# First chunks of x and w1 in three transfers, two chunks multiplied term by term, and a mask loaded from GpSimd's queue

## The chip, the cores and the metric

The program runs on one core of a Trainium2 chip. The metric is the device time of one execution in microseconds, as the median of several runs. The core has five engines that run their own instruction streams and wait for each other by semaphores: TensorE (PE, matrix products; PEld is its weight load), VectorE (DVE), ScalarE (ACT), GpSimd (POOL) and SyncE (SP), which here only issues transfers. Sixteen DMA engines move the data.

## The reference

With x of 2048 rows and 448 columns, the block mixes a linear attention and a squared-ReLU network by a gate of each row:

```python
g = sigmoid((x * gate_w).sum(-1, keepdims=True))
# A: 16 heads of 28 columns; phi(t) = where(t > 0, t + 1, exp(t)) + 1e-6
q, k, v = heads(x @ wqkv)
kv, z = sum_s phi(k)[s] v[s]^T, sum_s phi(k)[s]
a = ((phi(q) @ kv) / (phi(q) @ z + 1e-6)) @ wo
# B: 448 -> 1792 -> 448
b = relu(x @ w1 + b1) ** 2 @ w2 + b2
out = g * a + (1 - g) * b
```

## The kernel before, in words

Each operand of a product is split into a high part (a copy to PE's 32-bit type `fp32r`, `split_hi`) and a low part (the rest, a subtraction, `split_lo`), and a product is the sum of three terms: high by high, high of w1 by low of x, low of w1 by high of x. The 448 rows of the contraction are cut into four chunks of 128 rows; the last chunk holds the same 64 rows twice, so that two terms do for it.

The hidden layer is computed transposed: a tile of 128 hidden units (f) by 512 rows of x (a block b) needs 11 matmuls of 512 columns, three for each of chunks 0 to 2 and two for chunk 3. The first four tiles (`first`, f = 0 to 3 of block 0) are filled side by side, chunk by chunk, in lines 537 to 560, while x and w1 are still arriving. Everything after that is a long hand-written order on PE, ACT and DVE (`manual_schedule`): tiles of the up projection, of the down projection, key products, sums over keys, and in the second half the queries and the attention. `up_chunk` writes the three terms of one tile and one chunk; its last argument picks a single term.

The start goes like this. PE runs 14 matmuls on constants (line 177) whose result nobody reads. SP issues two transfers `xwr` of 256 KB, each with 256 columns of x's chunk 0 and 256 columns of w1's chunk 0, then x and w1 of chunks 1, 2 and 3 in turn, 256 KB each (`xr`, `w1r`), then biases and further weights. Of chunk 0, ACT makes the high part of x and DVE that of w1, half by half; PE multiplies halves of 256 columns of x with the first two tiles of w1 (line 547), then tiles 2 and 3 with all 512 columns, then the other two terms. Chunks 1 to 3 are split whole by ACT (high) and DVE (low), and PE does all terms of a tile before the next tile.

Transfers take their destinations from one ring of 15 slots (`slot`), and a transfer waits until the slot's last user is done. SP's transfers also take turns on eight semaphores, so that each waits for the landing of the eighth before it. Near the middle, `key_sums` builds `zk` on POOL and `load_kv` loads a mask `kvm` and four pieces of wv on SP's queue; `kv_product` needs the mask in line 406. POOL's own queue carries the rearranging transfers `qr` (line 474) and `m_s`.

Of the kernel before, what the change touches and what calls it, by code (L numbers as in the profile page):

```python
# [7 lines left out]
F = mybir.dt.float32  # L8
# [7 lines left out]
P = 128  # L16
TB = 512
# [8 lines left out]
def f32(ap):  # L26
    return ap.bitcast(F)


@with_exitstack  # L30
def gated_mix_kernel(ctx: ExitStack, tc: tile.TileContext, xw, xt, xn, wk, wq, wv, wo, w1a, w1b, w2, b1, b2, gw,
                     hmask, kvmask, halves, out):
    nc = tc.nc
    act, dve, pool, pe, sp = nc.scalar, nc.vector, nc.gpsimd, nc.tensor, nc.sync
# [13 lines left out]
    def bank(name):  # L48
        turn[0] ^= 1
        return ms_p.tile([P, 512], F, name=name, tag=f"ms{turn[0]}")  # L50
# [3 lines left out]
    def slot(shape, dt, name):  # L54
        return work.tile(shape, dt, name=name, tag="s", bufs=NSLOT)

    def load(dst, src):
        sp.dma_start(out=dst, in_=src)
# [4 lines left out]
    def split_hi(eng, hi, src):  # L63
        if eng is act:
            act.activation(hi, src, AF.Copy)  # L65
        elif eng is pool:
            pool.tensor_scalar(hi, src, 1.0, 0.0, op0=ALU.mult, op1=ALU.add)
        else:
            eng.tensor_copy(hi, src)  # L69

    def split_lo(eng, lo, src, hi):
        eng.tensor_tensor(lo, src, f32(hi), op=ALU.subtract)  # L72
# [29 lines left out]
    x_raw, xs = {}, {}  # L102
# [5 lines left out]
    def new_x(b):  # L108
        return [keep.tile([P, 4, TB], R, name=f"x{p}{b}", tag=f"x{p}", bufs=2) for p in "hl"]

    def split_x(b, c):
        if c == 0:
            xs[b] = new_x(b)
        (xh, xl), r = xs[b], x_raw[b, c]
        if c < 3:
            split_hi(act, xh[:, c], r)
            split_lo(dve, xl[:, c], r, xh[:, c])
        else:
            split_last(xh[:, 3], xl[:, 3], r, side)
# [9 lines left out]
    w1_s, w1_raw = {}, {}  # L129
# [5 lines left out]
    def new_w1(h, g):  # L135
        n, a, z = ((TB, 0, 16), (3 * P, 48, 0))[g]
        w = keep.tile([P, a + 7 * n + z], R, name=f"w1_{h}{g}", tag=f"w1{g}", bufs=1)
        w1_s[h, g] = w[:, a:a + 7 * n].rearrange("p (c n) -> p c n", c=7)
        return w1_s[h, g]

    def split_w1(h, g, c):
        if c == 0:
            new_w1(h, g)
        split_w(w1_s[h, g], c, w1_raw.pop((h, g, c)), act, dve)
# [7 lines left out]
    def split_w2(f):  # L152
        w2_s[f] = keep.tile([P, 2, D], R, name=f"w2_{f}", tag="w2", bufs=NH)
        split_hi(act, w2_s[f][:, 0], w2_raw[f])
        split_lo(dve, w2_s[f][:, 1], w2_raw.pop(f), w2_s[f][:, 0])
# [26 lines left out]
    dve.memset(side[64:], 1.0)  # L182

    xw_raw = []
    for n in range(2):
        xw_raw.append(slot([P, TB], F, f"xwr{n}"))
        load(xw_raw[n], xw[n])
    for c in range(1, 4):
        load_x(0, c)
        load_w1(0, 0, c)  # L190
# [27 lines left out]
    def up_chunk(ps, b, f, c, only=None):  # L218
        h, fl = divmod(f, NH)
        g, i = divmod(fl, 4)  # L220
        w, cols = w1_s[h, g], slice(i * P, (i + 1) * P)
        xh, xl = xs[b]
        if c < 3:
            terms = [(w[:, c, cols], xh[:, c]), (w[:, c, cols], xl[:, c]), (w[:, 4 + c, cols], xh[:, c])]
        else:
            terms = [(w[:, 3, cols], xh[:, 3]), (w[:, 3, cols], xl[:, 3])]
        for n, (a, m) in enumerate(terms):
            if only in (None, n):
                pe.matmul(ps, a, m, start=(c == 0 and n == 0), stop=(c == 3 and n == 1))  # L229
# [155 lines left out]
    kv, wv_s, kvm = [], [], []  # L385

    def load_kv(c):
        if c == 0:
            kvm.append(slot([JE, D], F, "kvm"))
            load(kvm[0], kvmask)  # L390
        wv_s.append(slot([P, D], F, f"wv{c}"))
        load(wv_s[-1], wv[c])

    def kv_product():
        kv_ps = bank("kv_ps")
        z_ps = mm_p.tile([P, 512], F, name="z_ps", tag="mm")
        for c in range(4):
            pe.matmul(z_ps[:, 2 * c:2 * c + 2], zks[0][:, c].rearrange("p j r -> p (j r)"), ones, start=True,  # L398
                      stop=True)
        dve.tensor_copy(zc, z_ps[:, 0:8:2])  # L400
        for j in range(NJ):
            js = slice(j * JE, (j + 1) * JE)
            for c in range(4):
                pe.matmul(kv_ps[:JE, js], wv_s[c][:, js], gsum[c][:, js], start=(c == 0), stop=(c == 3))  # L404
        raw = slot([JE, D], F, "kv_raw")
        dve.tensor_tensor(raw, kv_ps[:JE, :D], kvm[0], op=ALU.mult)
        return raw.rearrange("p (j k) -> p j k", j=NJ)
# [126 lines left out]

    first = [mm_p.tile([P, 512], F, name=f"h_ps0_{f}", tag="mm") if f < 2 else bank(f"h_ps0_{f}") for f in range(4)]
    for c in range(4):
        if c == 0:
            xs[0] = new_x(0)  # L540
            w, (xh, xl) = new_w1(0, 0), [x[:, 0] for x in xs[0]]
            sides = slice(0, TB // 2), slice(TB // 2, TB)
            for n, cols in enumerate(sides):
                split_hi(act, xh[:, cols], xw_raw[n][:, sides[0]])
                split_hi(dve, w[:, 0, cols], xw_raw[n][:, sides[1]])
                for f in range(2):
                    pe.matmul(first[f][:, cols], w[:, 0, f * P:(f + 1) * P], xh[:, cols], start=(n == 0), stop=False)  # L547
            for m, (lo, hi) in enumerate(((xl, xh), (w[:, 4], w[:, 0]))):
                for n, cols in enumerate(sides):
                    split_lo(dve, lo[:, cols], xw_raw[n][:, sides[m]], hi[:, cols])  # L550
        else:
            split_x(0, c)
            split_w1(0, 0, c)
        if c == 0:
            for n in range(3):
                for f in range(0 if n else 2, 4):
                    up_chunk(first[f], 0, f, c, n)
        else:
            for f in range(4):
                up_chunk(first[f], 0, f, c)  # L560
    split_w2(0)
    split_w2(1)
    wk_s = keep.tile([P, 7, D], R, name="wk_s", tag="wkm", bufs=1)
# [53 lines left out]
    for b in range(1, NB):  # L617
        for f in range(NH):
# [36 lines left out]
            if b == 2:  # L655
# [4 lines left out]
                if f == 5:  # L660
                    raw = slot([P, P], F, "hmr")
# [3 lines left out]
            if b == 3:  # L665
                if f < 4:
                    load_w1(1, 0, f)
                if f == 4:
                    for c in range(4):
                        split_w1(1, 0, c)  # L670
                if f >= 2:
                    load_w2(NH + f - 2)
                if f >= 3:
                    split_w2(NH + f - 3)
                if f == 5:
                    key_sums()
                if f >= 5:
                    load_kv(2 * f - 10)
                    load_kv(2 * f - 9)
# [5 lines left out]
    for n, b in enumerate(order):  # L685
        then = order[n + 1] if n + 1 < NB else None
        for f in range(NF - NH, NF):
# [43 lines left out]
            if n == 0:  # L731
                if fl < 4:
                    todo += queries(b, (3, 0, 1, 2)[fl])
                if fl == 0:
                    for c in range(4):
                        load_w1(1, 1, c)
                    raw = kv_product()
# [91 lines left out]
```

## Time and profile before

| | us |
|---|---|
| Median of 3 runs | 435.63 (435.18 to 436.45) |
| Profiled execution, own time | 435.59 |
| Its span in the trace | 433.8 |
| PE busy | 429.5 (99% of the span) |
| DVE, ACT, POOL busy | 283.7, 174.5, 72.1 |

The trace's span begins with the first instruction of the program; the profiled execution's time is 1.8 us longer than its span. Matmuls are pipelined: a row's length holds its tail as well, so the pace of PE is read from the distance between starts, not from the length of a row.

### The profile page before, as it was taken

Reading aid. Unit: us, or ns where it says so; the run is one execution under the profiler, and the core shown is the slowest. Engines: PE = TensorE matmul, PEld = TensorE weight load, DVE = VectorE, ACT = ScalarE, POOL = GpSimd, SP = SyncE. Lnnn points to the kernel's source line nnn. Section 1 sums busy time; section 2 is a strip of 40 time slices with the busy share of each in tenths; the row PEclk is TensorE's granted clock in tenths of the full one; section 3 lists DMA queues with packets and bytes.
Section 4 is the critical chain, followed back from the end, with each engine's and each line's share of the span. In section 5 each row is a group of like instructions: output and inputs, shape, how many; then the busy total and the mean of one; then the engine's idle time right before and its main releaser. Section 6 shows DMA issues by size and latency. Waiting matters only on the chain.

```text
span 433.8 us, 5561 instructions
## 1 busy us (share of the span) xinstructions
PE 429.5 (99%) x2052; PEld 381.4 (88%) x2052; DVE 283.7 (65%) x462; ACT 174.5 (40%) x302; POOL 72.1 (17%) x93
## 2 busy tenths in 40 slices
PE   9999999999999999999999999999999999999996
PEld 7898999898989899898898888988888888888986
DVE  5899518843499437784449777887653967457624
ACT  6865324421346122453145443444433434233421
POOL 0045006500065002540010441000100001000000
PEclk9999999999999999999999999999999999999999
DMA  7741302020221211223244321130101301002002
GB/s 282 240 134 51 109 0 69 27 68 1 70 82 65 72 45 48 65 58 111 63 118 134 69 65 38 61 122 0 26 0 48 136 0 26 0 0 86 0 2 85
DMA packets 18347, 29.00 MB, mean 67 GB/s; under 512 B 2896, under 2 KB 12672, under 8 KB 18320
## 3 DMA queue, kind: packets, MB, share of 16 engines
q1 hardware_dynamic: 16416, 26.35, 19.5%
q0 software_dynamic: 1760, 2.20, 2.3%
q8 instruction: 16, 0.26, 0.3%
q14 instruction: 11, 0.09, 0.1%
q10 hardware_dynamic: 144, 0.10, 0.1%
HBM read 22.31 MB, written 3.67 MB: 60 GB/s over the span
## 4 chain that ended last, share of the span: by engine, by line
PE 98%; DMA 1%; DVE 0%; ACT 0%; DVEq 0%; issue 0%
PE h_ps L229 32%; PE o_ps L254 31%; PE q_ps L84 8%; PE k_ps L254 8%; PE a_ps L84 8%; PE g_ps L84 8%; PE kv_ps L404 1%; DMA xwr<-in_xw 1%; PE m_ps L84 1%; PE d_ps L84 0%; PE h_ps L547 0%; PE z_ps L398 0%; DVE out L278 0%; ACT xh L65 0%; DVEq L825 0%
## 5 line engine op out<-in xcount | busy, mean ns | idle before, releaser
L254 PE MATMUL o_ps<-w,hh 128*128 128x448 f32 x448 | 128.6, 362 | 0.0
L229 PE MATMUL h_ps<-xh,w 128*128 128x512 f32 x390 | 124.8, 391 | 0.0
L254 PEld LDWEIGHTS o_ps<-w,hh 128*128 128x128 f32 x448 | 84.0, 187 | 7.7
L229 PE MATMUL h_ps<-xl,w 128*128 128x512 f32 x224 | 87.0, 391 | 0.0
L229 PEld LDWEIGHTS h_ps<-xh,w 128*128 128x128 f32 x390 | 73.4, 188 | 14.1
L254 PE MATMUL o_ps<-w,hl 128*128 128x448 f32 x224 | 81.2, 362 | 0.0
L233 ACT ACTIVATE hr<-h_ps,b_s 128x512 f32<-128x512 f32 x56 | 38.1, 680 | 86.1 <-PE h_ps L229 80.8
L69 DVE CAST hh<-hr 128x512 fp32r<-128x512 f32 x56 | 23.5, 420 | 61.8 <-ACT hr L234 61.7
L229 PEld LDWEIGHTS h_ps<-xl,w 128*128 128x128 f32 x224 | 42.4, 189 | 8.0
L254 PEld LDWEIGHTS o_ps<-w,hl 128*128 128x128 f32 x224 | 42.0, 188 | 3.7
L72 DVE TENSOR_TENSOR hl<-hr,hh 128x512 fp32r<-128x512 f32 x56 | 39.7, 709 | 3.3
L72 POOL TENSOR_TENSOR nl<-xnr,nh 128x384 fp32r<-128x384 f32 x16 | 17.2, 1076 | 119.0 <-ACT nh L65 118.9
L234 ACT ACTIVATE hr<-hr 128x512 f32<-128x512 f32 x56 | 35.4, 632 | 1.8
L84 PE MATMUL q_ps<-xh,wq_s 128*128 128x512 f32 x100 | 33.1, 390 | 0.0
L84 PE MATMUL a_ps<-m_s,qh 128*128 128x448 f32 x112 | 32.7, 362 | 0.0
L254 PE MATMUL k_ps<-wk_s,xh 128*128 128x448 f32 x112 | 32.7, 361 | 0.0
L474 POOL DMA_DIRECT2D qr<-qv x16 | 7.9, 503 | 124.3 <-ACT qv L471 94.5
L72 DVE TENSOR_TENSOR pl<-r,ph 128x448 fp32r<-128x448 f32 x16 | 23.7, 1479 | 0.0
L327 POOL TENSOR_TENSOR ksum<-ksum,r 128x448 f32<-128x448 f32 x15 | 23.3, 1555 | 1.1 <-DVE r L289 1.1
L84 PE MATMUL q_ps<-xl,wq_s 128*128 128x512 f32 x60 | 23.4, 389 | 0.0
L254 PE MATMUL k_ps<-wk_s,xl 128*128 128x448 f32 x64 | 23.2, 363 | 0.0
L84 PE MATMUL a_ps<-m_s,ql 128*128 128x448 f32 x64 | 23.2, 362 | 0.0
(111 smaller groups left out, 565.8 us busy)
## 6 DMA issues: line engine op xcount, KB each, us to landing
xr<-in_xt SPq DMA_DIRECT2D x27, 256.0 KB, 2.7
xnr<-in_xn SPq DMA_DIRECT2D x16, 224.0 KB, 2.5
out<-out SPq DMA_DIRECT2D x15, 224.0 KB, 1.9
w2r<-in_w SPq DMA_DIRECT2D x14, 224.0 KB, 2.7
w1r<-in_w1a SPq DMA_DIRECT2D x7, 256.0 KB, 2.7
w1r<-in_w1b SPq DMA_DIRECT2D x8, 192.0 KB, 3.3
m_s<-m POOLq DMA_DIRECT2D x12, 112.0 KB, 2.5
wqr<-in_wq SPq DMA_DIRECT2D x4, 256.0 KB, 2.7
```

What stands on the lines that cost most here:

```text
L69: eng.tensor_copy(hi, src)
L72: eng.tensor_tensor(lo, src, f32(hi), op=ALU.subtract)
L84: pe.matmul(out_ps, a, b, start=(i == 0), stop=(i == n - 1))
L229: pe.matmul(ps, a, m, start=(c == 0 and n == 0), stop=(c == 3 and n == 1))
L233: act.activation(r, ps, AF.Relu, bias=b1_s[:, f:f + 1])
L234: act.activation(r, r, AF.Square)
L254: pe.matmul(ps, a, m, start=start, stop=stop)
L327: pool.tensor_tensor(ksum, ksum, p, op=ALU.add)
L404: pe.matmul(kv_ps[:JE, js], wv_s[c][:, js], gsum[c][:, js], start=(c == 0), stop=(c == 3))
L474: pool.dma_start(out=r[p + 16:p + 32], in_=v[p:p + 16])
```

## The change

The first 512 KB now come in three transfers. The first two carry 256 columns of x and 128 columns of w1 each (192 KB), the third the other 256 columns of w1 (128 KB). DVE makes the high part of x, ACT that of w1, in pieces of 128, 128 and 256 columns. The four products of 256 columns are taken tile by tile and no longer half by half. Of chunk 1, x's high part moves from ACT to DVE, w1's high part is made on ACT in two halves, and PE goes through chunk 1 term by term over the four tiles. The mask `kvm` is issued by POOL and no longer by SP.

```diff
-    for n in range(2):
-        xw_raw.append(slot([P, TB], F, f"xwr{n}"))
-        load(xw_raw[n], xw[n])
+    for n, src in enumerate((xw0, xw1, w1c)):
+        xw_raw.append(slot([P, src.shape[1]], F, f"xwr{n}"))
+        load(xw_raw[n], src)
...
-            load(kvm[0], kvmask)
+            pool.dma_start(out=kvm[0], in_=kvmask)
...
-            sides = slice(0, TB // 2), slice(TB // 2, TB)
-            for n, cols in enumerate(sides):
-                split_hi(act, xh[:, cols], xw_raw[n][:, sides[0]])
-                split_hi(dve, w[:, 0, cols], xw_raw[n][:, sides[1]])
-                for f in range(2):
-                    pe.matmul(first[f][:, cols], w[:, 0, f * P:(f + 1) * P], xh[:, cols], start=(n == 0), stop=False)
-            for m, (lo, hi) in enumerate(((xl, xh), (w[:, 4], w[:, 0]))):
-                for n, cols in enumerate(sides):
-                    split_lo(dve, lo[:, cols], xw_raw[n][:, sides[m]], hi[:, cols])
+            hx = TB // 2
+            xcols, wcols = (slice(0, hx), slice(hx, TB)), (slice(0, P), slice(P, 2 * P), slice(2 * P, TB))
+            for n in range(2):
+                split_hi(dve, xh[:, xcols[n]], xw_raw[n][:, :hx])
+                split_hi(act, w[:, 0, wcols[n]], xw_raw[n][:, hx:])
+            split_hi(act, w[:, 0, wcols[2]], xw_raw[2])
+            for f, n in ((0, 0), (0, 1), (1, 0), (1, 1)):
+                pe.matmul(first[f][:, xcols[n]], w[:, 0, wcols[f]], xh[:, xcols[n]], start=(n == 0), stop=False)
+            for n in range(2):
+                split_lo(dve, xl[:, xcols[n]], xw_raw[n][:, :hx], xh[:, xcols[n]])
+            for n, raw in enumerate((xw_raw[0][:, hx:], xw_raw[1][:, hx:], xw_raw[2])):
+                split_lo(dve, w[:, 4, wcols[n]], raw, w[:, 0, wcols[n]])
+        elif c == 1:
+            (xh, xl), w, rx, rw = xs[0], w1_s[0, 0], x_raw[0, 1], w1_raw.pop((0, 0, 1))
+            split_hi(dve, xh[:, 1], rx)
+            for cols in (slice(0, 2 * P), slice(2 * P, TB)):
+                split_hi(act, w[:, 1, cols], rw[:, cols])
+            split_lo(dve, xl[:, 1], rx, xh[:, 1])
+            split_lo(dve, w[:, 5], rw, w[:, 1])
         else:
             split_x(0, c)
             split_w1(0, 0, c)
-        if c == 0:
-            for n in range(3):
-                for f in range(0 if n else 2, 4):
-                    up_chunk(first[f], 0, f, c, n)
-        else:
-            for f in range(4):
-                up_chunk(first[f], 0, f, c)
+        for n in range(3) if c < 2 else (None,):
+            for f in range(2 if (c, n) == (0, 0) else 0, 4):
+                up_chunk(first[f], 0, f, c, n)
```

On the host, `xw0` and `xw1` are the first and second 256 columns of x's chunk beside the first and second 128 columns of w1's, and `w1c` is columns 256 to 511 of w1's.

PE, from the last of chunk 0's terms into chunk 1, before (`h_ps_0` to `h_ps_3` are the four tiles, `xh` and `xl` x's high and low part, `w_00` both parts of w1):

```order
L229 MATMUL h_ps_2_167<-xh_169,w_00_171 128x512
L229 MATMUL h_ps_3_168<-xh_169,w_00_171 128x512
L229 MATMUL h_ps_0_165<-xh_169,w_00_171 128x512
L229 MATMUL h_ps_0_165<-xl_170,w_00_171 128x512
L229 MATMUL h_ps_0_165<-xh_169,w_00_171 128x512
L229 MATMUL h_ps_1_166<-xh_169,w_00_171 128x512
L229 MATMUL h_ps_1_166<-xl_170,w_00_171 128x512
```

The same place on PE now:

```order
L229 MATMUL h_ps_2_169<-xh_171,w_00_173 128x512
L229 MATMUL h_ps_3_170<-xh_171,w_00_173 128x512
L229 MATMUL h_ps_0_167<-xh_171,w_00_173 128x512
L229 MATMUL h_ps_1_168<-xh_171,w_00_173 128x512
L229 MATMUL h_ps_2_169<-xh_171,w_00_173 128x512
L229 MATMUL h_ps_3_170<-xh_171,w_00_173 128x512
L229 MATMUL h_ps_0_167<-xl_172,w_00_173 128x512
L229 MATMUL h_ps_1_168<-xl_172,w_00_173 128x512
```

Chunk 1's low part of w1, which was needed by the third of its matmuls, is now needed by the ninth.

DVE, from its first real work to chunk 1, before:

```order
L69 CAST w_00_171<-xwr_110 128x256
L69 CAST w_00_171<-xwr_112 128x256
L72 TENSOR_TENSOR xl_170<-xwr_110,xh_169 128x256
L72 TENSOR_TENSOR xl_170<-xwr_112,xh_169 128x256
L72 TENSOR_TENSOR w_00_171<-xwr_110,w_00_171 128x256
L72 TENSOR_TENSOR w_00_171<-xwr_112,w_00_171 128x256
L72 TENSOR_TENSOR xl_170<-xr_1_114,xh_169 128x512
L72 TENSOR_TENSOR w_00_171<-w1r_116,w_00_171 128x512
```

The same place on DVE now:

```order
L69 CAST xh_171<-xwr_110 128x256
L69 CAST xh_171<-xwr_112 128x256
L72 TENSOR_TENSOR xl_172<-xwr_110,xh_171 128x256
L72 TENSOR_TENSOR xl_172<-xwr_112,xh_171 128x256
L72 TENSOR_TENSOR w_00_173<-xwr_110,w_00_173 128x128
L72 TENSOR_TENSOR w_00_173<-xwr_112,w_00_173 128x128
L72 TENSOR_TENSOR w_00_173<-xwr_114,w_00_173 128x256
L69 CAST xh_171<-xr_1_116 128x512
L72 TENSOR_TENSOR xl_172<-xr_1_116,xh_171 128x512
L72 TENSOR_TENSOR w_00_173<-w1r_118,w_00_173 128x512
```

The two casts are now of x, one subtraction became three, and the cast of x's second chunk stands ahead of its subtraction.

POOL around the mask, in the middle of the program, now (before, the row of `kvm` stood on SP and the others stood here as they do):

```order
L327 TENSOR_TENSOR ksum<-ksum,r_1754 128x448
L376 MEMSET zk 128x128
L377 COPY zk<-ksum 128x384
L378 COPY zk<-ksum 128x4x16
L390 DMA kvm<-in_kvmask 112x448
L474 DMA qr_3_2012<-qv_2013 16x512 x4
```

Behind the mask on POOL's queue stand the four `qr` transfers.

## Rows read from the trace of the kernel before

**Rows 1.** The page: engines, then the chain that ended last.

```profile
PE 429.5 (99%) x2052; PEld 381.4 (88%) x2052; DVE 283.7 (65%) x462; ACT 174.5 (40%) x302; POOL 72.1 (17%) x93
...
PE 98%; DMA 1%; DVE 0%; ACT 0%; DVEq 0%; issue 0%
```

**Rows 2.** All waits of PE, whole span: us in total, times, longest.

```profile
PE warm_ps L177 <- PEq L821: 0.8, 1, 0.8
```

**Rows 3.** Timeline of PE: start us, length us, what; several alike are merged.

```profile
0.78 3.15 PE L177 MATMUL warm_ps<-const-bfloat16-1.0 128*128 128x256 bf16 x14 [0.78 <-PEq L821]
3.98 1.39 PE L547 MATMUL h_ps<-xh,w 128*128 128x256 f32 x4
5.17 1.05 PE L229 MATMUL h_ps<-xh,w 128*128 128x512 f32 x2
6.02 1.38 PE L229 MATMUL h_ps<-xl,w 128*128 128x512 f32 x4
7.24 1.31 PE L229 MATMUL h_ps<-xh,w 128*128 128x512 f32 x5
8.38 0.39 PE L229 MATMUL h_ps<-xl,w 128*128 128x512 f32 x1
8.61 0.62 PE L229 MATMUL h_ps<-xh,w 128*128 128x512 f32 x2
9.06 0.39 PE L229 MATMUL h_ps<-xl,w 128*128 128x512 f32 x1
...
15.41 0.57 PE L254 MATMUL k_ps<-wk_s,xh 128*128 128x448 f32 x2
```

**Rows 4.** Busy us of PE, PEld, DVE, ACT, POOL by stretch; then clock, DMA, GB/s.

```profile
0.00:3.98 3.98, 3.15 (x14) 1.90 (x14) 0.51 (x5) 1.70 (x2) 0.34 (x5) 1.00 0.42 150
3.98:6.64 2.66, 2.66 (x8) 2.28 (x9) 1.65 (x6) 1.04 (x2) 0.00 (x0) 1.00 0.94 326
```

**Rows 5.** Timeline of ACT; in brackets its idle time before, and what ended it.

```profile
3.51 0.42 ACT L65 ACTIVATE xh<-xwr 128x256 fp32r<-128x256 f32 x1 [1.49 <-DMA xwr<-in_xw]
4.11 0.42 ACT L65 ACTIVATE xh<-xwr 128x256 fp32r<-128x256 f32 x1 [0.18 <-DMA xwr<-in_xw]
5.96 0.63 ACT L65 ACTIVATE xh<-xr 128x512 fp32r<-128x512 f32 x1 [1.44 <-DMA xr<-in_xt]
6.66 0.63 ACT L65 ACTIVATE w<-w1r 128x512 fp32r<-128x512 f32 x1
...
14.25 0.69 ACT L233 ACTIVATE hr<-h_ps,b_s 128x512 f32<-128x512 f32 x1 [0.87 <-PE h_ps L229]
```

**Rows 6.** DMA issues on the page: kind, count, KB each, us to landing.

```profile
xr<-in_xt SPq DMA_DIRECT2D x27, 256.0 KB, 2.7
```

**Rows 7.** DMA to landing of `w1r`'s four 192 KB transfers, 205 to 225 us.

```profile
DMA to landing us min/median/max: 2.3/2.4/2.5
```

**Rows 8.** Groups of DVE, 0 to 14 us, by shape: busy us, mean ns.

```profile
L72 DVE TENSOR_TENSOR xl<-xr,xh 128x512 fp32r<-128x512 f32 x3 | 2.1, 693 | 0.9 <-ACT xh L65 0.9
L72 DVE TENSOR_TENSOR w<-xwr,w 128x256 fp32r<-128x256 f32 x2 | 0.8, 418 | 0.0
L69 DVE CAST w<-xwr 128x256 fp32r<-128x256 f32 x2 | 0.6, 296 | 2.7 <-DMA xwr<-in_xw 2.7
```

**Rows 9.** Timeline of SP, which issues the transfers.

```profile
0.74 0.85 SPq L58 DMA_DIRECT2D xwr<-in_xw  x2
1.64 0.43 SPq L58 DMA_DIRECT2D xr<-in_xt  x1
...
193.50 0.34 SPq L58 DMA_DIRECT2D kvm<-in_kvmask  x1
```

**Rows 10.** Timeline of POOL, then of DVE, around the mask.

```profile
192.82 0.70 POOL L378 COPY zk<-ksum 128x64 f32<-128x64 f32 x1
223.34 1.95 POOL L474 DMA_DIRECT2D qr<-qv  x4 [29.82 <-DVE kv_h L414]
...
221.33 0.62 DVE L406 TENSOR_TENSOR kv_raw<-kv_ps,kvm 112x448 f32<-112x448 f32 x1 [3.08 <-PE kv_ps L404]
```

More of the change, by code (lines that the diff above doesn't have):

```diff
@@ L30, in gated_mix_kernel @@
 @with_exitstack
-def gated_mix_kernel(ctx: ExitStack, tc: tile.TileContext, xw, xt, xn, wk, wq, wv, wo, w1a, w1b, w2, b1, b2, gw,
+def gated_mix_kernel(ctx: ExitStack, tc: tile.TileContext, xw0, xw1, w1c, xt, xn, wk, wq, wv, wo, w1a, w1b, w2, b1, b2, gw,
                      hmask, kvmask, halves, out):
@@ L801 @@
     a = {
-        "xw": np.stack([np.concatenate([t[:, n * TB // 2:(n + 1) * TB // 2] for t in (xt[0, 0], w1[0, 0])], axis=1)
-                        for n in range(2)]),
+        "xw0": np.concatenate([xt[0, 0, :, :TB // 2], w1[0, 0, :, :P]], axis=1),
+        "xw1": np.concatenate([xt[0, 0, :, TB // 2:], w1[0, 0, :, P:2 * P]], axis=1),
+        "w1c": w1[0, 0, :, 2 * P:TB],
         "xt": xt,
```

## The prediction

> **What bounds the kernel now.** I read the page first, then PE's waits, then the timelines of the first 16 us, because the change touches little else. PE is busy in 99% of the span and is 98% of the chain that ended last [rows 1], and of all its waits only the one before its first instruction is listed [rows 2]. So the kernel is one long stream of matmuls, and a change can gain or lose only in three ways: by when the stream of real products starts, by the pace at which PE runs, or by a hole in the stream. In the timeline of PE the first real product starts at 3.98 us; ahead of it are 14 matmuls on constants [rows 3]. In the same rows the reader is to see two paces. From 5.17 to 6.02 us two products of 512 columns take 0.85 us, 0.427 each; from 7.24 to 8.38 us five take 1.14 us, 0.228 each, and 8.38 to 8.61 is the same. 512 columns in 0.427 us are 1.2 GHz, the lower of PE's two levels; the 14 matmuls on constants (256 columns in about 0.213 us) run at it too. The four products from 6.02 to 7.24 take 1.22 us, so the clock rises among them, near 6.6 us. The windows print a granted clock of 1.00 for these stretches as well [rows 4], so here only the distance between starts tells the level. PE had then worked almost without a break since 0.78 us.
>
> **The sum, step by step, against the profiled execution (435.59 us, span 433.8; the median of the runs is 435.63).**
>
> *First product.* It waits for ACT's cast, which starts at 3.51 us when the first transfer has landed and takes 0.42 us [rows 5]; the landing is thus 2.75 us after the issue at 0.74 [rows 9]. The first transfer shrinks from 256 to 192 KB. The trace has no 192 KB transfer at the start; from below, 192 KB transfers land in 2.4 us later on [rows 7], from above 256 KB take 2.7 [rows 6], so the landing comes 0 to 0.3 us earlier. I take 0.15 to 0.3, as the smaller size should count. The casts: DVE's of 256 columns takes 0.30 us [rows 8]; ACT's of 128 columns is not in the trace, 0.42 for 256 and 0.63 for 512 columns [rows 5] put it on a line at 0.31, with 0.2 (half of 0.42) and 0.42 as ends. Product one could then start at about 3.6 us. But the last matmul on constants holds PE until about 3.72 us (0.78 plus 14 times 0.21) [rows 3], so the start is 3.72 to 3.9, 0.1 to 0.26 us earlier.
>
> *Products two to four.* The second cast of 256 columns started 0.60 us behind the first [rows 5]. With three quarters of the bytes I estimate 0.45, so the second transfer lands at 3.7 to 3.9 us, x's second half is cast by 4.0 to 4.2, and w1's second tile by ACT as soon. The four products, which ran from 3.98 to 5.17 us with two short stalls, now run from 3.72 to about 4.65 to 4.85, with one stall of about 0.2 us behind the first.
>
> *Tiles 2 and 3.* They need w1's other 256 columns from the third transfer. All 512 KB had landed by 4.11 us before [rows 5], and the third transfer completes the same 512 KB, with SP's issue of it at 1.64 us [rows 9]. Early end: 4.1 us, ACT's cast until 4.55, no wait. Late end: the next landing, that of x's chunk 1, came only at 5.96 us, 1.85 us behind the second and far more than the 0.7 to the one after it [rows 5]; the transfers have a slow stretch there, and the new third transfer may fall into it as the third did before. At 5.4 us (1.85 less the half of 0.7 that the smaller size saves, behind 3.9) the cast ends at 5.85 and tile 2 starts 0.7 us later than before. I take 4.1 to 4.6, nearer to the early end, because these bytes had landed by then before. Tile 2 then starts at 4.65 to 5.05 us instead of 5.17, 0.1 to 0.5 us earlier.
>
> *What that is worth.* If the clock rises at the same moment, a head start only moves products from the slow pace into the earlier time: each of 0.427 us of head start is one product more done by then, and it would have cost 0.228 later. So 0.1 to 0.5 us are worth 0.05 to 0.27; I take 0.2.
>
> *Chunk 1.* Before, w1's cast ended at 7.29 us [rows 5] and PE came to the chunk at about 8.15 (four products behind 7.24) [rows 3]: no wait. Now PE comes at about 7.95. x's cast on DVE (0.30 for 256 columns, 0.69 as the top for 512 [rows 8]) starts at 5.96, w1's first half is cast 0.42 us behind 6.66, at 7.08, the second at 7.5; the low part of w1 follows at 8.2 and is needed by the ninth product, at 9.8. So nothing waits, and the reorder by terms is worth nothing, below as above, as long as the data come 0.8 us ahead. ACT loses a cast of 0.63 us and pays 0.2 more for two halves; DVE gains about 0.4 us of work. DVE's next products for PE are chunk 2's, which PE reaches 12 products later, at 10.7 us; ACT's idle 0.87 us at 14.25, when it waits for PE's first tile [rows 5], is what is left of slack behind the chunks. The later transfers are issued one step of 0.47 us later each, while they land 0.7 us apart, so they lose nothing by it.
>
> *Mask.* On SP it was issued at 193.50 us [rows 9]; now POOL issues it behind the copies that end at 193.5 [rows 10]. Behind it on POOL stand only the `qr` transfers, at 223.34; DVE needs the mask at 221.33 and there waits for PE [rows 10]. Against 28 us of cover a landing of 2.5 us costs nothing; SP is free 0.4 us sooner, which nobody waits for. Only if POOL issued it behind the `qr` would it cost, and its order says otherwise.
>
> Sum: 435.59 - 0.2 = 435.4; from the median 435.63 it is 435.43. I forecast 435.4.
>
> **Two rules weighed.** The rows put 1.85, 0.7 and 0.6 us between landings of transfers issued 0.47 us apart [rows 5, 9]. The Trainium skill (DMA: Bandwidth & Descriptors, Anatomy of one DMA) gives each DMA about 2.0 us of fixed cost and advises one large transfer over several; by that an extra transfer that paid its fixed part alone would bring the third at 5.8 us, an estimate. The 0.6 and 0.7 us say that the fixed part overlaps, so I keep it to a rival. On the clock, PE worked from 0.78 us on and got the higher level near 6.6 [rows 3]. The skill (TensorE: Matmul & The Clock Gate, Part 1) says that the moment is not bound to the kernel's start and differs from run to run; the runs of before spread over 1.27 us, which fits, and no row here shows more.
>
> **Rivals.**
> - *No gain.* The landing does not depend on the size at 192 KB (2.75 us again), or the third lands near 4.7: tile 2 starts at 5.17 as before. For it: the page's median to landing of `xr` differs from 192 KB's by 0.3 us only. Time 435.6.
> - *Slower: the third transfer falls into the slow stretch.* PE has no work from 4.65 to 5.85 us. At the same clock rise that costs 0.7 times 0.228/0.427, 0.37 us: 436.0. It decides once the third lands after 4.75 us. Should the break also put off the rise of the clock, each further us at the lower level costs 0.47, and with 2 us more it is 436.9 and over the bound below. Against it: those bytes came by 4.11 before.
> - *Faster: the clock is high by the time of tile 2.* Then the whole head start counts, 0.5 us, and chunk 1 is reached so early that w1's halves and the order by terms count too: before, the third product needed w1's low part at about 8.0, now the ninth, worth some 0.4 us. Time 434.7. Against it: the level is low until 6.6 in the rows.
> - *The mask stalls POOL or DVE*: 28 us of cover speak against it.
>
> **Chances.** Forecast 0.65, no gain 0.15, slower 0.12, faster 0.07, mask 0.01. A measurement of this kernel tells 0.3% (1.3 us) from no change. The forecast and the no-gain case lie far within; of the slower rival about half passes the bound, with the mask 0.06; of the faster one only the part with a lucky clock, 0.04. Same 0.90. The range has the runs' own spread as its core: 435.18 less 0.5 to 436.45 less 0.05, that is 434.7 to 436.4, widened by 0.1 below.
>
> **What would show it.** In the profile after: first L550 product at 3.7 to 3.9 us; a stall of about 0.2 us behind it; tile 2 by 5.05; no wait of PE in chunk 1; the first product of `k_ps`, at 15.41 us before [rows 3], 0.05 to 0.3 us earlier; the mask landed by 197 us. I am wrong if PE waits for `xwr`'s third transfer, if the slow pace lasts visibly longer than 6.6 us, or if PE gets a hole anywhere behind 16 us.

## The result and the profile after

The changed kernel took 436.0 us (median of 22 runs, 435.35 to 437.69), the kernel before, timed beside it, 435.61 (22 runs, 435.06 to 436.81). The ratio is 1.0016, with an interval of 1.0009 to 1.0022: slower, by 0.4 us in the median and 0.7 us in the mean (the ratio goes with the mean), where 0.2 us faster was forecast. The 22 times fall into two groups: 17 from 435.35 to 436.38 and 5 from 437.21 to 437.69, with nothing between. The profiled execution took 435.99 us, with a span of 434.2 against 433.8, so it belongs to the first group.

The page's engines and the chain that ended last hardly differ from [rows 1]:

```profile
PE 428.8 (99%) x2052; PEld 380.8 (88%) x2052; DVE 284.2 (65%) x464; ACT 174.1 (40%) x303; POOL 72.6 (17%) x94
...
PE 98%; DMA 1%; SPq 0%; DVE 0%; ACT 0%; DVEq 0%; issue 0%
```

PE is busy 0.7 us less, in a span 0.4 us longer. All waits of PE over the whole span (us in total, times, longest) tell where the 1.1 us are; the first row is new against [rows 2]:

```profile
PE h_ps L229 <- ACT w L65: 1.2, 1, 1.2
PE warm_ps L177 <- PEq L829: 0.8, 1, 0.8
```

PE's timeline (start, length, what) puts the wait in front of tile 2, to be read beside [rows 3]:

```profile
3.61 1.27 PE L550 MATMUL h_ps<-xh,w 128*128 128x256 f32 x4
6.07 0.73 PE L229 MATMUL h_ps<-xh,w 128*128 128x512 f32 x2 [1.18 <-ACT w L65]
6.64 1.08 PE L229 MATMUL h_ps<-xl,w 128*128 128x512 f32 x4
7.56 1.98 PE L229 MATMUL h_ps<-xh,w 128*128 128x512 f32 x8
...
15.72 0.57 PE L254 MATMUL k_ps<-wk_s,xh 128*128 128x448 f32 x2
```

The first product starts 0.37 us earlier than before, tile 2 0.90 us later (6.07 against 5.17). Four products from 6.64 to 7.56 are 0.23 us each: after the hole (PE's wait) it runs at 2.4 GHz at once, while before it stayed at 0.427 us until about 6.6. That gives back some 0.67 us (6.6 less 5.17 is 1.43 us at the lower level, 0.47 us lost in each), so the first `k_ps` comes only 0.31 us later than before. The hole did not bring that about: the records of the clock in the traces put the rise to the higher level at 6.64 us before and at 4.61 here, ahead of the hole (which lasts from 4.89 to 6.07). In other executions without a hole in front of tile 2 it came anywhere from 3.53 (e6) to 6.66 us (e5). At 0.47 us of time for each us this alone makes single executions differ by about 1 us, so the medians have to carry the comparison. ACT's timeline shows what tile 2 waited for, beside [rows 5]:

```profile
3.17 0.31 ACT L65 ACTIVATE w<-xwr 128x128 fp32r<-128x128 f32 x1 [1.15 <-DMA xwr<-in_xw]
3.65 0.31 ACT L65 ACTIVATE w<-xwr 128x128 fp32r<-128x128 f32 x1 [0.17 <-DMA xwr<-in_xw]
5.60 0.42 ACT L65 ACTIVATE w<-xwr 128x256 fp32r<-128x256 f32 x1 [1.64 <-DMA xwr<-in_w1c]
7.55 0.73 ACT L65 ACTIVATE w<-w1r 128x256 fp32r<-128x256 f32 x2 [1.54 <-DMA w1r<-in_w1a]
```

The first two transfers are there at 3.17 and 3.65 us, earlier than before (3.51, 4.11), the third only at 5.60. The issues of the first 7 us (KB each, median us to landing) say the same of the transfers; the smallest of the three took longest:

```profile
xwr<-in_xw SPq DMA_DIRECT2D x2, 192.0 KB, 2.4
xwr<-in_w1c SPq DMA_DIRECT2D x1, 128.0 KB, 3.9
```

The windows (us; busy time of PE, PEld, DVE, ACT and POOL; clock; share of the DMA engines; GB/s) show the stretch in which its last bytes went. After:

```profile
3.50:4.00 0.50, 0.50 (x4) 0.29 (x2) 0.35 (x2) 0.31 (x1) 0.00 (x0) 1.00 0.30 55
4.00:5.00 1.00, 0.89 (x4) 0.69 (x3) 1.00 (x4) 0.00 (x0) 0.00 (x0) 1.00 0.76 257
5.00:6.00 1.00, 0.00 (x0) 0.00 (x0) 0.01 (x1) 0.40 (x1) 0.00 (x0) 1.00 0.97 353
```

The same stretches before:

```profile
3.50:4.00 0.50, 0.44 (x3) 0.02 (x1) 0.29 (x1) 0.42 (x1) 0.00 (x0) 1.00 0.66 225
4.00:5.00 1.00, 1.00 (x4) 0.91 (x5) 0.89 (x4) 0.42 (x1) 0.00 (x0) 1.00 0.86 260
5.00:6.00 1.00, 1.00 (x4) 0.83 (x4) 0.74 (x3) 0.04 (x1) 0.00 (x0) 1.00 0.99 375
```

The slow stretch is in both: the rate is 260 and 257 GB/s between 4 and 5 us, 375 and 353 behind it; from 3.5 to 4.0 us it is far deeper after (55 against 225). Before, both transfers of chunk 0 had landed by 4.08 us; now some of what tile 2 needs lies in it. The rate alone does not say why the third is late. Of its 128 packets (1 KB each, one partition's row) the trace has 90 started by 4.0 us and 34 only after 4.5; two that started at 3.46 and 3.56 took 1.20 and 0.68 us, where the usual one takes 0.05. Meanwhile the packets of the next transfer were moving. So most of the third transfer was early, and a few late packets made its landing. It was the same in e8 and e11 below: half of its packets had ended by 3.53 and 3.43 us, the last at 5.23 and 5.30.

The mask, now issued by POOL, beside [rows 10] (timeline of POOL, then of DVE):

```profile
194.35 0.54 POOL L390 DMA_DIRECT2D kvm<-in_kvmask  x1 [0.52 <-ACT w L65]
223.63 1.95 POOL L474 DMA_DIRECT2D qr<-qv  x4 [28.74 <-DVE kv_h L414]
...
221.63 0.62 DVE L406 TENSOR_TENSOR kv_raw<-kv_ps,kvm 112x448 f32<-112x448 f32 x1 [3.08 <-PE kv_ps L404]
```

It landed 3.7 us behind its issue, at about 198 us, and is needed at 221.63, where DVE waits for PE, 3.08 us as before.

### The profile page after: what moved, and what is told of

Its sections match the earlier page's. It is cut to its first block, busy times and chain, and to the rows that moved or that the text cites. A ratio compares the mean times of both kernels' runs of the same rounds, so it can differ in the third digit from the quotient of the medians.

```text
span 434.2 us, 5568 instructions
## 1 busy us (share of the span) xinstructions
PE 428.8 (99%) x2052; PEld 380.8 (88%) x2052; DVE 284.2 (65%) x464; ACT 174.1 (40%) x303; POOL 72.6 (17%) x94
## 4 chain that ended last, share of the span: by engine, by line
PE 98%; DMA 1%; SPq 0%; DVE 0%; ACT 0%; DVEq 0%; issue 0%
PE h_ps L229 32%; PE o_ps L254 31%; PE q_ps L84 8%; PE a_ps L84 8%; PE k_ps L254 8%; PE g_ps L84 8%; DMA xwr<-in_w1c 1%; PE kv_ps L404 1%; PE m_ps L84 1%; PE d_ps L84 0%; SPq L58 0%; PE z_ps L398 0%; DVE out L278 0%; ACT w L65 0%; DVEq L833 0%
```

## The experiments

The theory: the third transfer falls into a slow stretch of the stream, PE gets a hole while its clock is still coming up, and in some executions the hole also puts off the rise of the clock, which makes the group above 437 us. The rivals: chunk 1 by terms, or x's cast on DVE, costs the time; or the stretch lies at a fixed time and has nothing to do with how the bytes are cut. Ratios are to the kernel before on the same chip.

**e1_two_transfers.** The changed kernel with the two transfers of before:

```diff
-    for n, src in enumerate((xw0, xw1, w1c)):
-        xw_raw.append(slot([P, src.shape[1]], F, f"xwr{n}"))
-        load(xw_raw[n], src)
+    for n in range(2):
+        xw_raw.append(slot([P, TB], F, f"xwr{n}"))
+        load(xw_raw[n], xw[n])
...
-                split_hi(act, w[:, 0, wcols[n]], xw_raw[n][:, hx:])
-            split_hi(act, w[:, 0, wcols[2]], xw_raw[2])
+                split_hi(act, w[:, 0, wcols[n]], xw_raw[0][:, hx + n * P:hx + (n + 1) * P])
+            split_hi(act, w[:, 0, wcols[2]], xw_raw[1][:, hx:])
```

> The changed kernel with the first 512 KB in two transfers of 256 KB again; casts, order by terms and mask stay as changed. Theory A, the loss is PE's wait for the third transfer in front of tile 2: no wait there, tile 2 starts by 5.1 us, 435.3 to 435.6 us. Theory B, the loss comes from the rest (casts on other engines, chunk 1 by terms, mask on POOL): 436.0 us as the changed kernel.

Measured: 435.1 us (11 runs, 434.65 to 435.6) against 435.47; ratio 0.999 (0.9981 to 0.9999). That is below the range of theory A, and tile 2 starts at 5.27 us and not by 5.1. PE's timeline has no hole in front of tile 2 (some 0.3 us are lost behind the first product):

```profile
3.95 1.52 PE L550 MATMUL h_ps<-xh,w 128*128 128x256 f32 x4
5.27 0.67 PE L229 MATMUL h_ps<-xh,w 128*128 128x512 f32 x2
```

With all else of the change kept, the loss is gone, and so is every time above 435.6. The loss belongs to the cut into three transfers.

**e2_transfers_alone.** The other half: the three transfers with the casts and products of chunk 0 that go with them; chunk 1 and the mask are as before. The edit is shown against the changed kernel:

```diff
-        elif c == 1:
-            ...
-        for n in range(3) if c < 2 else (None,):
+        for n in range(3) if c < 1 else (None,):
...
-            pool.dma_start(out=kvm[0], in_=kvmask)
+            load(kvm[0], kvmask)
```

> The kernel before with the three transfers and the casts and products of chunk 0 that go with them; chunk 1 and the mask as before. Theory A: PE waits about 1.2 us before tile 2, 436.0 us and now and then over 437. Theory B: 435.6 us.

Measured: 437.75 us (6 runs, 435.93 to 438.02, four of them above 437.7) against 435.47; ratio 1.0041 (1.0026 to 1.0057). The transfers alone lose, and more than the whole change does: theory A's direction holds, its 436.0 does not. Some 0.42 us of it have nothing to do with the start: in all four profiles of this kernel, and in e9's, the program ends that much later behind the last packet (1.69 us against 1.26 before and after). SP ends the program by checking its semaphores one after another, 0.06 us each. With 127 transfers on SP's queue (before, after) the last landing met the last check; with one more (e2, e9) it met the first of eight. Without it e2's ratio would still be about 1.003, an estimate. The profiled execution, though, was the quickest of the six, and its third transfer was in time (ACT's timeline):

```profile
4.15 0.42 ACT L65 ACTIVATE w<-xwr 128x256 fp32r<-128x256 f32 x1 [0.19 <-DMA xwr<-in_w1c]
6.13 0.63 ACT L65 ACTIVATE xh<-xr 128x512 fp32r<-128x512 f32 x1 [1.56 <-DMA xr<-in_xt]
6.99 0.63 ACT L65 ACTIVATE w<-w1r 128x512 fp32r<-128x512 f32 x1 [0.23 <-DMA w1r<-in_w1a]
```

So the landing differs from execution to execution: here 4.12 us, the value that I had taken, and the slow stretch falls on the next transfer. To catch an execution of the other group the same kernel was profiled three times more.

**e8_transfers_alone_again, e10_transfers_alone_third_look, e11_transfers_alone_fourth_look.** No edit against e2.

> The version before with the three transfers alone, once more, to see an execution near 437.7 us in a trace. Theory C: PE has a hole at tile 2 or in chunk 1 while its clock is still low, and the distance between starts stays at 0.427 us for 512 columns until well behind 7 us. Theory D: the clock rises by 6.7 us as in the other traces, and the holes alone add up to 2 us.

> The version before with the three transfers alone, again, to see an execution near 437.7 us in a trace. Theory C: a hole of PE near 5 us and a clock that rises only well behind 7 us. Theory D: the clock rises by 7 us and holes add up to 2 us.

> The version before with the three transfers alone once more. Theory C: in an execution near 437.7 us the clock rises only well behind 7 us. Theory D: it rises by 7 us and PE's holes add up to 2 us.

Measured: 436.4, 436.35 and 438.02 us. In e10 the third transfer landed at 3.95 us and there was no hole in front of tile 2; against the profile before it loses 0.11 us by `k_ps`, 0.20 between 275 and 286 us and the 0.42 at the end. In e8 it landed at 5.55, PE waited 1.33 us, and its pace behind the hole was 0.23 us:

```profile
6.04 0.73 PE L229 MATMUL h_ps<-xh,w 128*128 128x512 f32 x2 [1.33 <-ACT w L65]
6.60 1.09 PE L229 MATMUL h_ps<-xl,w 128*128 128x512 f32 x4
```

In e11 it landed at 5.57, and PE's timeline reads:

```profile
3.62 1.43 PE L550 MATMUL h_ps<-xh,w 128*128 128x256 f32 x4
6.06 1.22 PE L229 MATMUL h_ps<-xh,w 128*128 128x512 f32 x2 [1.02 <-ACT w L65]
7.08 1.91 PE L229 MATMUL h_ps<-xl,w 128*128 128x512 f32 x4
8.79 1.71 PE L229 MATMUL h_ps<-xh,w 128*128 128x512 f32 x5
10.34 0.40 PE L229 MATMUL h_ps<-xl,w 128*128 128x512 f32 x1
...
17.40 0.57 PE L254 MATMUL k_ps<-wk_s,xh 128*128 128x448 f32 x2
```

The same hole as in the changed kernel, but behind it four products take 1.71 us, 0.427 each, and of the next five (1.55 us) two more are slow: the lower level lasts from 6.06 to about 9.6 us. That is 3.6 us at a loss of 0.47 us each, 1.68; `k_ps` comes at 17.40 against 15.72 in the changed kernel's profile, 1.68 later. This is the group above 437 us, and theory C holds for it. Why e8 escaped is in the records of the clock: there the rise came at 4.15 us, ahead of the hole (from about 4.7), as in the changed kernel's profile; in e11 PE went into the hole at the lower level, and the rise came at 9.61.

**e5_keep_busy.** Is it the hole, or the late data, that puts off the rise? Six products on constants fill the hole of the changed kernel:

```diff
                 pe.matmul(first[f][:, xcols[n]], w[:, 0, wcols[f]], xh[:, xcols[n]], start=(n == 0), stop=False)
+            for _ in range(6):
+                pe.matmul(warm_ps[:, :256], warm[:, :P], warm, start=True, stop=True)
```

> The changed kernel with six more of the constant matmuls of 256 columns between the fourth product and tile 2, so that PE works on while it waits for the third transfer. Theory C, the executions over 437 us are those in which PE's hole puts off the rise of its clock: none over 436.9, median 435.7 to 436.1. Theory D, in those executions the third transfer is simply later still: about a fifth of them stay over 437, median 436.0 or more.

Measured: 435.83 us (12 runs, 435.59 to 436.13) against 435.29; ratio 1.0011 (1.0002 to 1.002). PE's timeline:

```profile
3.62 1.38 PE L550 MATMUL h_ps<-xh,w 128*128 128x256 f32 x4
4.80 1.50 PE L552 MATMUL warm_ps<-const-bfloat16-1.0 128*128 128x256 bf16 x6
5.95 1.03 PE L229 MATMUL h_ps<-xh,w 128*128 128x512 f32 x2
6.83 1.08 PE L229 MATMUL h_ps<-xl,w 128*128 128x512 f32 x4
```

The third transfer landed at 5.27 us here and its cast was done at 5.72; the idle products themselves hold PE until 5.95. So tile 2 is hardly earlier than in the changed kernel and a loss stays, and the clock rises at 6.66. But no run lies above 436.13, where 5 of 22 of the changed kernel and 5 of 9 of e2's kernel lie above 437.2. With e4 below, which keeps PE at work too, it is 0 of 23 against 10 of 31: by these counts the hole, and not the lateness, makes the second group.

**e6_terms_alone.** The kernel before with chunk 1 term by term and nothing else:

```diff
-        if c == 0:
-            ...
+        for n in range(3) if c < 2 else (None,):
+            for f in range(2 if (c, n) == (0, 0) else 0, 4):
+                up_chunk(first[f], 0, f, c, n)
```

> The kernel before with chunk 1 term by term and nothing else. If the order by terms is what makes the two-transfer version faster: 435.1 us. If it is worth nothing, as predicted: 435.5 us.

Measured: 435.26 us (12 runs, 434.61 to 436.26) against 435.29; ratio 0.9997 (0.9989 to 1.0006). The order is worth nothing that can be measured.

**e4_tiles01_first.** The changed kernel with work for PE that needs no third transfer: the other two terms of tiles 0 and 1 ahead of tiles 2 and 3.

```diff
+        if c == 0:
+            for fs in ((0, 1), (2, 3)):
+                for n in range(3):
+                    for f in fs if n or fs[0] else ():
+                        up_chunk(first[f], 0, f, c, n)
+            continue
...
```

> The changed kernel, but PE takes the low-part terms of tiles 0 and 1 ahead of tiles 2 and 3, so that four products which need nothing of the third transfer stand in front of the wait. Theory A: PE's wait before tile 2 shrinks from 1.2 us to 0 to 0.5 us, 435.2 to 435.6 us, and no run over 437. Theory B: 436.0 us.

Measured: 435.37 us (11 runs, 434.95 to 435.71) against 435.47; ratio 0.9998 (0.9989 to 1.0006). The third transfer landed at 5.64 us, yet PE's timeline has no hole:

```profile
3.63 1.37 PE L550 MATMUL h_ps<-xh,w 128*128 128x256 f32 x4
4.79 1.08 PE L229 MATMUL h_ps<-xl,w 128*128 128x512 f32 x2
5.67 1.51 PE L229 MATMUL h_ps<-xh,w 128*128 128x512 f32 x4
...
15.27 0.57 PE L254 MATMUL k_ps<-wk_s,xh 128*128 128x448 f32 x2
```

Real work in the hole takes away both parts of the loss. The early start of 0.35 us does not show in the median, whose interval reaches from 0.5 us faster to 0.3 slower; in this profile, where the clock rises at 6.60 us, much as in the one before (6.64), `k_ps` comes 0.14 us earlier.

**e3_third_on_act.** The third transfer on ACT's queue, so that it doesn't stand behind the other two:

```diff
-        load(xw_raw[n], src)
+        (act if n == 2 else sp).dma_start(out=xw_raw[n], in_=src)
```

> The changed kernel with the third transfer issued by ACT's queue instead of SP's. If it is late because it stands third on SP's queue, it lands by 4.3 us, tile 2 starts by 4.8 us and the time is 435.3 us. If all transfers go slowly between 3.6 and 5 us whatever their queue, or if it now takes its bytes from the first two, it lands after 5 us or the first product starts later than 3.7 us, and the time is 435.9 or more.

Measured: 435.27 us (11 runs, 434.78 to 436.64) against 435.47; ratio 0.9999 (0.9991 to 1.0008): the loss is gone here too, and neither expectation fits whole. The third landed at 3.60 us and tile 2 started at 4.92, but the casts behind the first two began 0.3 and 0.5 us later than in the changed kernel (3.47 and 4.11), and chunk 1's w1 landed at 7.46, hardly earlier than in the changed kernel (7.53). In PE's timeline the wait is there now:

```profile
3.91 0.37 PE L550 MATMUL h_ps<-xh,w 128*128 128x256 f32 x1
...
7.95 1.20 PE L229 MATMUL h_ps<-xh,w 128*128 128x512 f32 x4 [0.56 <-ACT w L65]
```

In this profile three transfers share the rate whichever queue they stand in: what one gains the others lose. The wait of 0.56 us takes back the early tile 2 (`k_ps` at 15.36). The execution's 435.94 us is above the median because of another pause, 0.41 us at 275 us.

**e7_all_later.** Does the stretch lie at a fixed time? Five memsets of the first destination hold back the whole stream; SP's order is written by hand, so that nothing passes it.

```diff
...
+        if n == 0:
+            for _ in range(5):
+                dve.memset(xw_raw[0], 0.0)
```

> The changed kernel with five memsets of the first destination in front of the first transfer, which put off all transfers by about 1.5 us; everything comes later, about 437 us. If the slow stretch of the transfers belongs to a fixed time after the start, it stays between 3.6 and 5 us and now hits the first two transfers. If it belongs to the place in the stream, it moves on by about 1.5 us and hits the third transfer or x's chunk 1 again, near 5.1 to 6.5 us.

Measured, one execution: 440.13 us, not 437, because the delay came out at 2.9 us and not 1.5 and the clock rose only at 11.85. SP's timeline, and ACT's cast behind the third transfer:

```profile
3.64 0.86 SPq L58 DMA_DIRECT2D xwr<-in_xw  x2
4.55 0.43 SPq L58 DMA_DIRECT2D xwr<-in_w1c  x1
...
8.45 0.42 ACT L65 ACTIVATE w<-xwr 128x256 fp32r<-128x256 f32 x1 [1.62 <-DMA xwr<-in_w1c]
```

Issued 2.9 us later, the third landed 2.9 us later (8.43), 3.9 us behind its issue, as in the changed kernel. Packets that take 0.5 us and more begin at 6.34 us here, at 3.46 in the changed kernel. In this one execution the stretch went with the stream and not with the time.

**e9_first_cut_in_two.** Is it always the third transfer? The first is cut into 128 and 64 KB, so that w1's last columns are the fourth.

```diff
-        load(xw_raw[n], src)
+        for cols in ((slice(0, 2 * P), slice(2 * P, 3 * P)) if n == 0 else (slice(None),)):
+            load(xw_raw[n][:, cols], src[:, cols])
```

> The changed kernel with the first transfer cut in two (128 KB of x, 64 KB of w1), so that the former second is now the third and the former third the fourth. If the late one is the third of SP's queue whatever its size, the transfer of 192 KB lands after 5 us, PE's second product waits for it, and the time is 436.5 us or more. If the late one is whatever is under way some 2.9 us behind the first issue, the first 384 KB land by 3.8 us as they did, the fourth transfer lands at 5 to 5.6 us, and the time is 436.0.

Measured, one execution: 437.46 us. Neither expectation came true: the third (192 KB) landed at 4.25 us, the fourth at 4.67, and the next, x's chunk 1, at 6.79. PE's timeline:

```profile
3.58 0.56 PE L551 MATMUL h_ps<-xh,w 128*128 128x256 f32 x1
4.63 1.01 PE L551 MATMUL h_ps<-xh,w 128*128 128x256 f32 x3 [0.49 <-DVE xh L69]
...
6.29 1.91 PE L230 MATMUL h_ps<-xl,w 128*128 128x512 f32 x4
8.00 2.65 PE L230 MATMUL h_ps<-xh,w 128*128 128x512 f32 x8
```

Four products from 6.29 to 8.00 are 0.427 us each, and the eight from 8.00 to 10.49 (2.49 us, where 1.82 would do) hold three slow ones more: the lower level until about 9.4 us (9.36 by the record of the clock), behind a wait of only 0.49. Of the time, 0.42 us are the late end told under e2.

**e12_two_transfers_by_halves.** e1 with the four products half by half, as before, so that the second half of x is needed later:

```diff
-            for f, n in ((0, 0), (0, 1), (1, 0), (1, 1)):
+            for f, n in ((0, 0), (1, 0), (0, 1), (1, 1)):
```

> The two-transfer version, with the four products of 256 columns in the order of before (both tiles with x's first half, then both with the second), so that the second product does not wait for the second transfer. If PE's hole of 0.3 us behind its first product is worth what a head start is worth at the lower clock, 0.1 to 0.15 us: 434.95 to 435.2 us. If not: 435.1 to 435.3 us as the two-transfer version.

Measured: 434.99 us (12 runs, 434.58 to 435.49) against 435.41; ratio 0.9989 (0.998 to 0.9997): the lowest median here and within the first expectation, though not clear of e1's 0.999. Its timeline of PE:

```profile
3.98 1.30 PE L550 MATMUL h_ps<-xh,w 128*128 128x256 f32 x4
5.08 0.65 PE L229 MATMUL h_ps<-xh,w 128*128 128x512 f32 x2
...
14.63 0.57 PE L254 MATMUL k_ps<-wk_s,xh 128*128 128x448 f32 x2
```

Of the 0.78 us by which `k_ps` is earlier than in [rows 3], tile 2 accounts for 0.09, the clock, high from 5.08 on, for some 0.67. The clock's moment differs between executions of one kernel too, so the medians count: 0.4 us. What gives e1 and e12 these 0.4 us is not settled; tile 2 is 0.10 later than before in the one and 0.09 earlier in the other, and e6 alone gives none.

## Why the prediction was wrong

**The step that failed is "Tiles 2 and 3".** "I take 4.1 to 4.6, nearer to the early end, because these bytes had landed by then before." The third transfer landed at 5.57 us. The late end that I had worked out beside it was nearly exact (landing 5.4, cast done 5.85, tile 2 0.7 us later; measured 5.57, 6.02, 0.90). The reason for the early end was wrong: that the same bytes had landed by 4.11 in two transfers says nothing of them in three, because the slow stretch lies behind the transfers that go first. It need not hit the third: landings at 3.95 (e10) and 4.12 (e2) stand beside 5.57 (after), 5.64 (e4), 5.27 (e5), 5.55 (e8) and 5.57 (e11). With such a spread, and a hole once the landing comes later than 4.75, the rival "slower: the third transfer falls into the slow stretch" deserved more than 0.12. Its price, 436.0, is the measured median, in part by luck: it was worked out for a tile 2 that is 0.7 us later under a clock that rises near 6.6. In the profiled execution tile 2 was 0.90 us later, worth 0.48 at that pace, but the clock had risen at 4.61, and the median has the five executions above 437 us in it.

**The rival's second half came true as well.** "Should the break also put off the rise of the clock" was priced at 0.47 us for each further us, 436.9 with 2 us. In e11 it was 3.6 us and 1.68 us of time. In the nine profiles in which PE had no wait of 0.4 us or more ahead of tile 2 (before, e1, e2, e3, e4, e5, e6, e10, e12) the clock rose between 3.53 and 6.66 us. In the four with one, and the stream at its usual time, it depends on which came first: the clock had risen before the hole in two (after at 4.61, e8 at 4.15), and the hole cost only its length; in the other two the hole came first (from 4.1 us in e9, from 5.0 in e11), and the rise came at 9.36 and 9.61. e5 ties the group to the hole. What sets the moment of the rise where there is no hole is not shown.

**First product:** 3.61 us against 3.72 to 3.9. The landing was earlier than taken (3.15, 2.4 us behind the issue at 0.74, the lower bound by [rows 7]), and the last product on constants didn't hold PE until 3.72. ACT's cast of 128 columns took 0.31 us, as on the line through its two sizes.

**Products two to four:** done by about 4.9 us against 4.65 to 4.85: the hole of 1.18 us ends at 6.07. Right in size, and of no use, since tile 2 was late. e4, which starts as early and has no hole, shows no gain either, so the 0.2 us that I took for the head start are not found in a median; e4's interval does not exclude them, and its profile has 0.14.

**Chunk 1:** right. PE doesn't wait there, and e6 gives 0.9997 for the order. But that the later transfers lose nothing was wrong: chunk 1's x and w1 landed at 6.90 and 7.53 us against 5.94 and 6.63 before, and w1's first half was cast from 7.55 on instead of 6.66. That cost nothing only because PE itself was late. In e2, e3 and e10, where the third transfer was in time and tile 2 0.37, 0.25 and 0.41 us early, PE waited 0.35 and 0.56 us in chunk 1 and in e10 lost some 0.3 there, and `k_ps` came 0.08 and 0.05 us earlier and 0.11 later than before. So the early end that I had chosen would not have given the forecast gain either.

**Mask:** right, no cost, though it took 3.7 us to land and not 2.5 (at 198.0 us, where I had said by 197); the cover of 23 us is what made that harmless.

**The rule weighed.** The Trainium skill (DMA: Bandwidth & Descriptors, Anatomy of one DMA) would have had the third at 5.8 us, an estimate, by a fixed cost paid in full; that section fits its figure to transfers issued by GpSimd, and these are SP's. It landed between 5.27 and 5.64 in five profiles, but at 3.95 and 4.12 in two, and the first two landings lie 0.48 us apart, so the fixed part isn't paid in turn here. The advice of the same page (Rules for kernel authors) to coalesce small transfers into a large one, with 64 KB named as small, points the same way: two transfers of 256 KB beat three, 0.999 against 1.0016. But it is not the number that costs here: e3 and e4 have three and stand at 0.9999 and 0.9998.

**Open.** The cause of the slow stretch, which is to say of the few packets that take 0.5 to 1.5 us. In e7 it moves with the stream; it falls on the third transfer or on the one behind it, and in one profile each isn't lifted by a second queue (e3) or by another cut (e9). Whether it is set by the bytes under way or by the number of transfers was not told apart, nor whether the shorter rows of the three transfers (1.5 and 1 KB instead of 2) matter. That e2's kernel has a larger share of executions above 437 us than the changed kernel (5 of 9 against 5 of 22) is not explained either.

## What to carry to other kernels

A transfer that is split so that a first part comes earlier also has a last part that comes later: ask what the engine does when the last part falls into the worst gap between landings that the trace shows anywhere near, and give that gap its own chance. Put work that needs only the first parts behind them, as e4 does, before moving any bytes. While PE's clock is still coming up, a hole can cost more than its own length; in e5, with idle products in the hole, none of 12 executions paid that part.

## What was not expected of the hardware

- 128 KB took 3.9 us to land where the 192 KB ahead of them took 2.4, in the same queue, with the DMA engines at 55 GB/s from 3.5 to 4.0 us; single packets of 1 KB took 1.20 and 0.68 us, the usual one 0.05.
- A wait of PE of 0.5 to 1.0 us that began at the lower level of the clock went along with that level until 9.4 and 9.6 us (e9, e11), 1.7 us of time in e11; waits of 1.2 and 1.3 us that began behind the rise (after, e8) did not bring it back.
- 196 KB issued by GpSimd landed in 3.3 to 3.7 us (eight profiles), the same from SP in 2.4 to 2.6 (six).
- One transfer more on SP's queue (e2, e9) made the end of the program 0.42 us longer, by the order in which SP checks its semaphores.
